# How the first tiles reach TensorE in a fused mixer kernel: layer norm by float32 products and DMA transposes, and w1 by column blocks

## The chip, the cores and the metric

The kernel runs on one core of a Trainium2 chip. The metric is the device time of one launch in microseconds (us), lower being better. Five engines work side by side, each through its own instructions in order: TensorE (PE) multiplies matrices, VectorE (DVE), ScalarE (ACT) and GpSimd (POOL) work elementwise, and SyncE (SP) issues DMAs. Waits between engines are semaphores.

## The reference, cut to what matters

```
x  = A_x                                # 1 x 2048 x 512, float32
xn = layernorm(x)
s  = A(xn)  # qkv = layernorm-ed input @ wqkv (512 x 1536); 32 heads of 16;
            # each position attends to 8 positions, 2 apart; then @ wo (512 x 512)
g  = silu(B(xn))
            # B: y = layernorm(xn); h = gelu(y @ w1 + b1)  (512 x 1376); h @ w2 + b2
out = x + s * g
```

## The kernel before, in words

**Tiles.** Positions are dealt into two classes of 1024, even and odd (the dilation is 2), each of eight tiles of 128 positions. Layer norm is by position, so a tile with positions on the partitions gets its mean and variance from DVE; but for a product with a weight the 512 features must be on the partitions. Each normalized tile is therefore transposed into `yT` (four tensors of four tiles: `yT[0]` and `yT[1]` for class 0, `yT[2]` and `yT[3]` for class 1).

**Precision.** A float32 product is done as three f16 products: every operand is split into a high f16 part and a low one (the remainder), and hi x hi, lo x hi and hi x lo are summed in PSUM. Weights are scaled by a power of two first, which needs a sum of squares over the whole weight (`sumsq`, on ACT), a sum over partitions (`total`, a product with a matrix of fours on PE), and a few tiny DVE steps (`half_exp`, `up`, `down`); then `split` writes the two halves (line 436 the high half on ACT or 434 on DVE, line 437 the low half on DVE).

**Stages.** The work is cut into eight units (class, block of eight heads). `qkv` (lines 611 to 666) multiplies the eight tiles of a class by a 384-column block of wqkv, 12 matmuls a tile (line 632), and ACT evicts each into `U[0]` or `U[1]` in turn (line 648). `attention` (676 on) is DVE and POOL work on `U`. The MLP (`mlp1`, 890 to 932, and `mlp2`, 934 on) runs over four chunks of 512 positions and eleven column blocks of w1 and is spread between the units. Last comes the product with wo (837 on).

**The start.** Tiles of x are loaded in the order of `LOADS` (line 40), between the two halves of wqkv's first block. `ln0` (540 to 583) takes a group of tiles: statistics (`stats`, 525 and 526), the factors (`factors`, 504 to 520, with a power on POOL at 512 and 519), the normalized tile (by DVE at 564 or by ACT at 534), four PE transposes of 128 x 128 into PSUM (571), and copies into the high and low halves of `yT` (581 on ACT, 582 on DVE). Tiles 2 and 3 (`FP`, line 42) also leave a float32 copy (577), and in unit 0 they are multiplied as float32 by the wqkv block as it was loaded (639), so that these products need not wait for its scale. Up to 26 idle matmuls (1042) fill PE before that.

**w1 and w2.** w1 (512 x 1376) lies as four row blocks side by side, [128, 4 x 1376]. It is loaded in four pieces (`W1C`, line 34) from SP's queue, before anything of w2; each is split as a whole (1083 to 1086), with both halves on DVE. A column block of `mlp1` reads from all four row blocks, so its 12 matmuls need all four pieces. w2 follows in two loads of 1 MiB and three of 256 KB (1024 to 1029).

**What sets the order.** The program doesn't run in the order of its text. Every operation is handed to a planner (class `Plan`, line 83) with an engine, an estimated duration, what it reads and writes, and a priority (a lower number first). The planner plays the engines in estimated time (`issue`, line 203): at each step it takes, for the engine that can start earliest, the ready operation of the lowest priority, and this gives each engine's fixed order. Buffers come from rings (`Ring`); a new user waits for the last. Estimates for DMAs are in `place`, and `earliest` limits the planned DMAs in flight. On the chip an engine that reaches a wait in its order holds everything behind it.

Of the kernel before, what the change touches and what calls it, by code (L numbers as in the profile page):

```python
# [33 lines left out]
W1C = [0, 2048, 4096, 5120, KT * F]  # L34
LAG = 2
# [17 lines left out]

DVE_LO = range(0, 44)

# [27 lines left out]
class Plan:  # L83
# [76 lines left out]
    def earliest(self, o):  # L160
        t = max(self.free[o.eng], o.ready)
        if o.port:
            t = max(t, self.portfree)
        if o.eng == "sp" and o.nbytes and len(self.landed) >= QUEUE:
            t = max(t, self.landed[-QUEUE])
        return t

    def place(self, o, t):

        if o.eng == "sp":  # L170
# [6 lines left out]
            self.landed.append(end)  # L177
# [79 lines left out]
MARGIN = {"pe": 0.2, "dve": 0.15, "act": 0.05}  # L257
# [3 lines left out]
QUEUE = 8  # L261

PW2, PS2 = 0.9, 0.74
PWQ1, PW1 = 0.7, 0.75
# [4 lines left out]
WAKE = 4  # L269
WAKE0 = 22  # L270
# [6 lines left out]
PFP = 0.62  # L277
# [13 lines left out]
def tile_mixer(ctx, tc, a_x, a_wqkv, a_wo, b_w1, b_b1, b_w2, out):  # L291
# [34 lines left out]
    ident = sb.tile([P, P], F32, name="ident")  # L326
    make_identity(nc, ident)
    fours = sb.tile([P, P], F32, name="fours")
    nc.vector.memset(fours, 4.0)
    halves = sb.tile([P, 16], F32, name="halves")  # L330
# [8 lines left out]
    w1 = sb.tile([P, 2, KT, F], F16, name="w1")  # L339
# [18 lines left out]
    R_w = Ring(sb, [P, 16], F32, 8, "lw")  # L358
# [27 lines left out]
    def total(dst, dkey, cols, n, ckeys, late=False):  # L386

        b = (R_ps if late else R_z[0]).new()
        if n == 2:
            for k in range(2):  # L390
                pl.add("pe", 0.15, lambda k=k: nc.tensor.matmul(
                    b.t[:, 0:1], fours, cols()[:, k:k + 1], start=(k == 0), stop=(k == 1)),
                    [ckeys[k]], [b], prio=min(pl.prio, PTOT))
            n = 1
        else:
            pl.add("pe", 0.3, lambda: nc.tensor.matmul(b.t[:, 0:n], fours, cols()[:, 0:n], start=True,
                                                       stop=True), ckeys, [b], prio=min(pl.prio, PTOT))
# [62 lines left out]
    def prep_q(hb):  # L460
# [9 lines left out]
        with pl.fuse():  # L470
# [4 lines left out]
            down(qsc[:, hb, 1:2], ("qi", hb), h, 24.0)  # L475
        st = 1 if hb == 0 else 2
# [14 lines left out]
    cpos = [2, 3, 0, 1, 4, 5, 6, 7]  # L491
# [46 lines left out]
    yF = {}  # L538

    def ln0(ii, xs, xkeys):  # L540
        n = len(ii)
        first, way = dict(prio=PLN + pl.prio * 1e-3), dict(prio=PLN + 0.03 + pl.prio * 1e-3)
# [4 lines left out]
        behind = [("yd", i) for i in (2, 3) if n > 1]  # L547
        fz = pl.fuse()
        for a in range(n - 1):
            with pl.fuse():  # L550
                stats(mv, a, mk[a], xs[a], [xkeys[a]] + behind)
        fz.__enter__()
        stats(mv, n - 1, mk[n - 1], xs[n - 1], [xkeys[n - 1]] + behind)
        rb = factors(n, mv, mk, cT[:, 0, cpos[ii[0]]:cpos[ii[0]] + n], [("c", 0, i) for i in ii],
                     ii[0] in ACT_Y, lambda: fz.__exit__(None, None, None), **{"pp": first["prio"]})
        for a, i in enumerate(ii):
            y = R_f.new()
            o = (i % 4) * P
            dst = yT[i // 4]
            if ii[0] in ACT_Y:  # L560
                with prio(PLN + 0.04):
                    y_act(xs[a], rb, a, [xkeys[a]], lambda y=y: y.t, y, ("y_", i))
            else:
                dve(512, lambda a=a, y=y: nc.vector.tensor_scalar(
                    y.t, xs[a](), mv()[:, a, 0:1], rb[0].t[:, a:a + 1], op0=ALU.subtract,
                    op1=ALU.mult), [xkeys[a], (rb[0], 0)] + mk, [y, ("yd", i)], f=0.72, **first)
            b = R_z[1 + i % 3].new()

            def tr(b=b, y=y):
                for k in range(KT):  # L570
                    nc.tensor.transpose(b.t[:, k * P:(k + 1) * P], y.t[:, k * P:(k + 1) * P], ident)
            pe(4, P, tr, [y], [b], fp32=2, **first)
            p3 = lambda b=b: b.t.rearrange("p (k t) -> p k t", k=KT)
            hi, lo = dst[:, 0, :, o:o + P], dst[:, 1, :, o:o + P]
            if i in FP:
                yf = yF[i] = R_L.new()
                act(512, lambda b=b, yf=yf: nc.scalar.copy(yf.t, b.t), [b], [yf], aps=0, **way)
                p3, b, way2 = (lambda yf=yf: yf.t.rearrange("p (k t) -> p k t", k=KT)), yf, dict(prio=PFP)
            else:
                way2 = way  # L580
            act(512, lambda p3=p3, hi=hi: nc.scalar.copy(hi, p3()), [b], [("yh", 0, i)], aps=0, **way2)
            dve(512, lambda p3=p3, hi=hi, lo=lo: nc.vector.tensor_tensor(  # L582
                lo, p3(), hi, op=ALU.subtract), [b, ("yh", 0, i)], [("y", 0, i)], port=i in FP, **way2)

# [651 lines left out]
```

## Time and profile before

| | |
|---|---|
| median of 3 runs | 420.26 us (419.76 to 420.91) |
| the profiled execution | 419.94 us, span 418.2 us from first to last instruction |
| PE busy | 408.5 us, 98% |
| DVE busy | 384.2 us, 92% |
| ACT, POOL busy | 214.8 us, 111.4 us |
| moved by DMA | 44.83 MB, mean 107 GB/s |

An engine's row in the profile gives its busy time; a group of instructions is a line of the kernel, an engine, and output <- input tiles with buffer numbers left out (`ps`, `z` and `pl` are PSUM; `f`, `prod`, `lw`, `s` small SBUF rings). A float32 matmul shows as two instructions, each with its own weight load. In the timeline each row is a start, a length, the engine, the line and how many instructions were merged; brackets give the idle time before it and what ended it. A PE row's length holds the way through the pipeline, so the distance between starts is what a row costs. SPq rows are DMA issues; their landing is given apart.

### The profile page before, as it was taken

The numbers are of one execution on the slowest core, as the hardware profiler recorded it, in microseconds if no ns is written. First come the engines' busy times: TensorE is split into PE (matmuls) and PEld (weight loads), VectorE is DVE, ScalarE is ACT, GpSimd is POOL, SyncE is SP. The second block draws the span as 40 slices with busy tenths as digits, with TensorE's granted clock in tenths as the row PEclk, the third lists the DMA queues.
The fourth block names the chain that finished last, engine by engine and source line by source line (L and its number), as shares of the span: only waits on it lengthen the run. The fifth ranks groups of instructions, "written<-read, shape, count | busy, mean of one in ns | idle before, by whom it ended". The sixth has DMA issues, their size and how long they took to land.

```text
span 418.2 us, 5558 instructions
## 1 busy us (share of the span) xinstructions
PE 408.5 (98%) x2095; PEld 208.7 (50%) x2095; DVE 384.2 (92%) x403; ACT 214.8 (51%) x321; POOL 111.4 (27%) x126
## 2 busy tenths in 40 slices
PE   7799999999999999999999999999999999999995
PEld 4466544444554455445544654465455544444442
DVE  5958999999999999899998999999999998999953
ACT  6799972762539764843396335134212573263500
POOL 5310200004341525042504250433124304520031
PEclk9999999999999999999999999999999999999999
DMA  8963260030036247621271025104505343016132
GB/s 292 415 225 106 77 213 2 16 137 0 0 97 175 72 100 171 135 59 27 71 206 63 2 87 125 52 26 130 184 0 152 117 130 119 2 34 217 27 125 100
DMA packets 42650, 44.83 MB, mean 107 GB/s; under 512 B 27480, under 2 KB 27920, under 8 KB 42112
## 3 DMA queue, kind: packets, MB, share of 16 engines
q1 hardware_dynamic: 42624, 44.49, 35.1%
q8 instruction: 16, 0.26, 0.3%
q14 instruction: 10, 0.08, 0.1%
HBM read 23.53 MB, written 7.34 MB: 74 GB/s over the span
## 4 chain that ended last, share of the span: by engine, by line
PE 81%; DVE 11%; ACT 4%; issue 1%; DMA 1%; SPq 0%; POOL 0%; DVEq 0%
PE ps L632 24%; PE z L943 24%; PE ps L898 22%; PE ps L815 7%; PE z L815 2%; DVE w L437 2%; DVE prod L691 2%; DVE L L694 2%; ACT w L436 1%; DMA prod<-in_A_x_dram 1%; DVE bn L525 1%; PE pl L632 1%; DVE h L921 1%; PE pl L815 1%; DVE w L434 1%
## 5 line engine op out<-in xcount | busy, mean ns | idle before, releaser
L898 PE MATMUL ps<-yT,w 128*128 128x512 f16 (+1 forms) x528 | 120.8, 379 | 0.0
L632 PE MATMUL ps<-wq,yT 128*128 128x384 f16 x708 | 117.9, 326 | 1.0 <-DVE yT L582 1.0
L943 PE MATMUL z<-w,h 128*128 128x512 f16 x480 | 110.8, 379 | 0.0
L632 PEld LDWEIGHTS <-yT 128*128 128x128 f16 x744 | 72.8, 98 | 49.0 <-DVE yT L582 1.3
L898 PEld LDWEIGHTS <-w 128*128 128x128 f16 (+1 forms) x528 | 52.9, 100 | 61.3 <-issue 0.5
L915 ACT ACTIVATE ps<-ps,b1T,hsc 128x512 f32<-128x512 f32 (+1 forms) x44 | 32.8, 748 | 87.1 <-PE ps L898 86.9
L691 DVE TENSOR_TENSOR prod<-U 128x2048 f32<-128x2048 f32 x32 | 73.0, 2285 | 2.8 <-DMA U<-U 1.7
L943 PEld LDWEIGHTS <-h 128*128 128x128 f16 x480 | 47.0, 98 | 55.4
L694 DVE TENSOR_REDUCE L<-prod 128x128 f32<-128x2048 f32 x32 | 72.9, 2280 | 0.4
L648 ACT ACTIVATE U<-ps,cs 128x384 f32<-128x384 f32 x61 | 35.1, 578 | 65.1 <-PE ps L632 63.6
L749 DVE TENSOR_TENSOR prod<-pl,U 128x2048 f32<-128x2048 f32 x28 | 63.2, 2281 | 4.3 <-POOL prod L759 4.2
L759 POOL TENSOR_TENSOR prod<-prod,prod 128x2048 f32<-128x2048 f32 x7 | 31.7, 4528 | 100.0 <-DVE prod L749 100.0
L769 POOL TENSOR_TENSOR prod<-prod 128x1024 f32<-128x1024 f32 x14 | 32.9, 2347 | 0.0
L768 POOL COPY gate<-prod 1x1 f32<-1x1 f32 x21 | 5.5, 263 | 92.7 <-DVE prod L691 89.9
L815 PE MATMUL ps<-wo,oT 128*128 128x512 f16 x132 | 29.6, 379 | 0.0
L921 DVE SCALAR_TENSOR_TENSOR h<-ps,hsc,h 128x512 f16<-128x512 f32 x40 | 29.5, 741 | 0.1
L815 PEld LDWEIGHTS <-oT 128*128 128x128 f16 x189 | 18.5, 98 | 22.1
L918 ACT ACTIVATE h<-ps,hsc 128x512 f16<-128x512 f32 x40 | 27.2, 683 | 0.8
L744 DVE TENSOR_TENSOR prod<-prod,prod 128x2048 f32<-128x2048 f32 x9 | 20.5, 2278 | 0.0
L915 ACT ACT_TABLE_LOAD x11 | 14.1, 1283 | 6.1 <-PE ps L898 5.9
L769 POOL TENSOR_TENSOR prod<-prod,prod 128x1024 f32<-128x1024 f32 x7 | 16.4, 2348 | 0.0
L732 ACT ACTIVATE o<-prod,osc 128x1024 f16<-128x1024 f32 (+1 forms) x9 | 9.5, 1052 | 11.8 <-POOL prod L769 7.4
(155 smaller groups left out, 346.8 us busy)
## 6 DMA issues: line engine op xcount, KB each, us to landing
f<-in_A_x_dram SPq DMA_DIRECT2D x31, 256.0 KB, 3.2
U<-U SPq DMA_DIRECT2D x16, 392.0 KB, 3.8
gd<-f SPq DMA_DIRECT2D x12, 256.0 KB, 2.2
oT<-in_B_w_dram SPq DMA_DIRECT2D x2, 1024.0 KB, 11.9
yT<-in_B_w_dram SPq DMA_DIRECT2D x2, 1024.0 KB, 12.6
f<-gd SPq DMA_DIRECT2D x8, 256.0 KB, 3.2
out_dram<-f SPq DMA_DIRECT2D x8, 256.0 KB, 2.6
out_dram<-U SPq DMA_DIRECT2D x7, 256.0 KB, 2.0
```

The source lines that it names most:

```text
L632: nc.tensor.matmul(b.t[:, 0:384], y[:, s, k, o:o + P], wq[:, hb, t, k], start=(n == 0), stop=(n == 11))
L648: act(384, lambda i=i, b=b: nc.scalar.activation(U3[:, i:i + 31:15, :], b.t[:, 0:384].rearrange("p (t e) -> p t e", t=3), AF.Identity, sca ...
L691: dve(2048, lambda p2=p2, g=g: nc.vector.tensor_tensor(p2(), q, slots(Ut, KH, 2 * g), op=ALU.mult), qk + [("kh", ub, 0), ("kh", ub, 1), (" ...
L694: dve(2048, lambda pr=pr, g=g: nc.vector.tensor_reduce(L3()[:, 2 * g:2 * g + 2], pr.t.rearrange("p (r f d) -> p r f d", r=2, d=DH), AX.X, ...
L749: dve(2048, lambda: nc.vector.tensor_tensor(pr.t.rearrange("p (r f d) -> p r f d", r=2, d=DH), A3()[:, 2 * g:2 * g + 2].rearrange("p r (f ...
L759: pool(4.75, lambda: nc.gpsimd.tensor_tensor(acc.t, acc.t, p1.t, op=ALU.add), [acc, p1], [acc])
L769: nc.gpsimd.tensor_tensor(x.t[:, 0:1024], x.t[:, 0:1024], y(), op=ALU.add)
L815: nc.tensor.matmul(b.t, oT[:, hb, i // 4, s, i % 4], wo[:, t, hb], start=(hb == 0 and n == 0), stop=(hb == last and n == 2))
L898: nc.tensor.matmul(b.t[0:M], w1[:, s, k, f * P:f * P + M], yT[ch][:, t, k], start=(n == 0), stop=(n == 11))
L915: act(512, lambda: nc.scalar.activation(b.t[0:M], b.t[0:M], AF.Gelu_apprx_tanh, bias=b1T[0:M, f:f + 1], scale=hsc[0:M, 1:2]), [b, ("b1T",) ...
L921: dve(512, lambda: nc.vector.scalar_tensor_tensor(lo()[0:M], b.t[0:M], hsc[0:M, 2:3], hi()[0:M], op0=ALU.mult, op1=ALU.subtract), [b, hk], ...
L943: nc.tensor.matmul(z.t, hl[s][0:K, t * P:(t + 1) * P], w2[0:K, w, f], start=(f == 0 and n == 0), stop=(f == NF - 1 and n == 2))
```

## The change

The host passes a further input, `A_xt`: tiles 4 to 7 of class 0 with the features already on the partitions, 256 KB each. The loads become t4, t5, the two halves of wqkv's first block, x0, x1, t6, x2, x3, t7, x4 to x7 (t for a transposed tile, x for a plain one; all eight plain tiles are still loaded, one at a time).

`FP` is now (4, 5, 6, 7). For each of these, `center` sums a transposed tile over its four row blocks (DVE for tiles 4 and 5, POOL for 6 and 7), takes the mean over the partitions by a float32 product with a matrix of 1/512, and subtracts it in place on DVE. `direct` multiplies the centred tile as float32 by the unscaled wqkv block, four matmuls of 384 columns each. The factor 1/standard deviation is not applied to the tile: it is put into the scale `cs` of the eviction in unit 0.

For all eight tiles `y0` makes the normalized tile in place (ACT for tiles 0, 2, 3, 4, DVE for 1, 5, 6, 7), casts its high half (on the same engine), subtracts for the low half on DVE, and SP issues a DMA transpose of both halves into `yT`. The PE transposes, their identity matrix and the copies out of PSUM are gone. Unit 0 takes the tiles in the order 4, 5, 6, 7, 0, 1, 2, 3, of which 0 to 3 are f16 products from `yT`; the other units take 1 to 7 and then 0.

w1 lies as eleven column blocks one after another, each with its four row blocks inside. It is still loaded in four pieces, now issued by ACT: piece n after the transpose of tile n has landed. It is split in seven parts (`W1P`): the first two of one column block each, with the high half on DVE; then five with the high half on ACT, with a priority behind the MLP's own steps. A column block of `mlp1` waits for its own part alone. w2's two large loads are issued by ACT after the transposes of tiles 5 and 7.

`total` uses bf16 matrices of fours and the upper 16 bits of the sums. The planner limits planned DMAs in flight by bytes instead of by number, and several priorities are renamed or moved. A branch for the MLP's low half that no step took (lines 927 to 931) and its diagonal matrix (1081) are removed.

```diff
-GROUPS = [(2,), (3,), (0, 1), (4, 5), (6, 7)]
-LOADS = [(2, 1), "q0", "q2", (3, 1), (0, 2), (4, 2), (6, 2)]
-FP = (2, 3)
-ACT_Y = (0, 1, 4, 5)
-W1DVE = (0, 1, 2, 3)
+W1P = [(0, 1), (1, 2), (2, 4), (4, 6), (6, 8), (8, 10), (10, 11)]
+W1FIRST = 2
+FP = (4, 5, 6, 7)
+XC = FP
+GROUPS = [(0, 1), (2, 3), (4, 5, 6, 7)]
+LOADS = [("t", 4), ("t", 5), ("q", 0), ("q", 2), ("x", 0), ("x", 1), ("t", 6), ("x", 2), ("x", 3), ("t", 7),
+         ("x", 4), ("x", 5), ("x", 6), ("x", 7)]
+XT = (0, 4, 30, 34)
+Y_ENG = {0: "act", 1: "dve", 2: "act", 3: "act", 4: "act", 5: "dve", 6: "dve", 7: "dve"}
+W1ENG = ["dve", "dve", "act", "act", "act", "act", "act"]
...
+    mean1 = sb.tile([P, P], F32, name="mean1")
+    nc.vector.memset(mean1, 1.0 / D)
...
+    xt = {i: U[1][:, XT[n] * P:(XT[n] + 4) * P].rearrange("p (k t) -> p k t", k=KT) for n, i in enumerate(FP)}
+    def center(i):
...
+        if n < 2:
+            dve(512, lambda: nc.vector.tensor_reduce(f3()[:, 0], x3.rearrange("p k t -> p t k"), AX.X, ALU.add),
+                [("xt", i)], [f], port=False)
+        else:
+            pool(0.75, lambda: nc.gpsimd.tensor_tensor(f3(), x3[:, 0:2], x3[:, 2:4], op=ALU.add), [("xt", i)], [f])
+            pool(0.45, lambda: nc.gpsimd.tensor_tensor(f3()[:, 0], f3()[:, 0], f3()[:, 1], op=ALU.add), [f], [f])
+        pe(1, P, lambda: nc.tensor.matmul(b.t[:, 0:P], mean1, f3()[:, 0], start=True, stop=True), [f], [b], fp32=6, prio=0.04)
+        m = lambda: b.t[:, 0:P].rearrange("p (o t) -> p o t", o=1).to_broadcast([P, KT, P])
+        dve(512, lambda: nc.vector.tensor_tensor(x3, x3, m(), op=ALU.subtract), [b, ("xt", i)], [("xc", i)], port=False)
...
+    def direct(i):
+        b = pb[i] = (([R_pl] + R_z[1:] + [R_ps] * 4)[FP.index(i)]).new()
+        for k in range(KT):
+            pe(1, 384, lambda k=k: nc.tensor.matmul(
+                b.t[:, 0:384], xt[i][:, k], stq[0]()[:, k * 384:(k + 1) * 384], start=(k == 0), stop=(k == KT - 1)),
...
+    def y0(i, a, mv, mk, rb):
...
+        dma(P * 2048, lambda: nc.sync.dma_start_transpose(
+            dst.rearrange("p a k t -> p (a k) t")[:, :, o:o + P], y16.t.bitcast(F16)),
+            [y16, (y16, 0)], [("yh", 0, i), ("y", 0, i)], rate=1e6, issue=1.3, tail=2.6)
...
-    IORD, IORD0 = [2, 3, 1, 4, 5, 6, 7, 0], [2, 3, 0, 1, 4, 5, 6, 7]
+    IORD, IORD0 = [1, 2, 3, 4, 5, 6, 7, 0], [4, 5, 6, 7, 0, 1, 2, 3]
...
-                nc.tensor.matmul(b.t[0:M], w1[:, s, k, f * P:f * P + M], yT[ch][:, t, k],
+                nc.tensor.matmul(b.t[0:M], w1[:, s, f * 512 + k * M:f * 512 + (k + 1) * M], yT[ch][:, t, k],
...
+    def behind(nbytes, fn, r, w):
+        pl.add("act", 0.4, fn, r, w, nbytes=nbytes)
...
+            behind(P * 4 * (b - a), lambda a=a, b=b: nc.scalar.dma_start(s1[n]()[:, a:b], b_w1[:, W1C[n] + a:W1C[n] + b]),
+                   [W1AFTER[n]], [key])
...
+    W1AFTER = [("y", 0, 0), ("y", 0, 1), ("y", 0, 2), ("y", 0, 3)]
...
+        behind(P * 8192, lambda: nc.scalar.dma_start(s2a, b_w2[:, 0:4]), [("y", 0, 5)], [("yT", 2), ("s2", 0)])
+        behind(P * 8192, lambda: nc.scalar.dma_start(s2b, b_w2[:, 4:8]), [("y", 0, 7)], [("yT", 3), ("s2", 1)])
...
+    lay["A_xt"] = inputs["A_x"].reshape(P, NI, DIL, KT, P)[:, list(FP), 0].transpose(1, 3, 2, 0)
...
+    w1 = inputs["B_w1"].reshape(KT, P, F)
+    lay["B_w1"] = _np.concatenate([w1[:, :, f * P:(f + 1) * P].transpose(1, 0, 2).reshape(P, -1) for f in range(NF)], 1)
```

More of the change, by code (lines that the diff above doesn't have):

```diff
@@ L275 @@
 PQLO = 0.55
-PFP = 0.62
+PFPLN = 0.35
 U1MH = 4
@@ L545, in ln0 @@
         mk = [(mvb, a) for a in range(n)]
-        behind = [("yd", i) for i in (2, 3) if n > 1]
-        fz = pl.fuse()
-        for a in range(n - 1):
+        for a, i in enumerate(ii):
             with pl.fuse():
[L551 to L555, printed above, removed]
@@ L636, in qkv @@
             if u == 0 and i in FP:
-                yf = yF[i]
-                for k in range(KT):
-                    pe(1, 384, lambda k=k, b=b, yf=yf: nc.tensor.matmul(
-                        b.t[:, 0:384], yf.t[:, k * P:(k + 1) * P], stq[hb]()[:, k * 384:(k + 1) * 384],
-                        start=(k == 0), stop=(k == KT - 1)), [yf, ("stq", hb, k)], [b], fp32=4.1,
-                       holds=stkey[hb], after=pl.users([b] + [("v", ub, i)]))
                 ends = []
```

246 lines of the change are left out of this document (130 added, 116 removed).

## The prediction

> **What bounds the kernel now.** I read the page's busy line and chain first, then the busy time by stage, cut at 20.70 us, where TensorE (PE) last waited.
>
> ```profile
> span 418.2 us, 5558 instructions
> PE 408.5 (98%) x2095; PEld 208.7 (50%) x2095; DVE 384.2 (92%) x403; ACT 214.8 (51%) x321; POOL 111.4 (27%) x126
> PE 81%; DVE 11%; ACT 4%; issue 1%; DMA 1%; SPq 0%; POOL 0%; DVEq 0%
> ```
>
> ```profile
> 5.80:20.70 14.90, 11.59 (x55) 6.72 (x55) 13.40 (x49) 12.07 (x23) 5.19 (x7) 1.00 1.03 402
> 20.70:48.74 28.04, 28.04 (x182) 18.04 (x183) 20.60 (x46) 27.35 (x50) 3.71 (x3) 1.00 0.37 128
> 48.74:400.62 351.88, 351.54 (x1778) 175.18 (x1776) 341.23 (x289) 172.89 (x247) 94.18 (x100) 1.00 0.32 91
> ```
>
> The columns are the stretch, its length, then busy us of PE, PEld, DVE, ACT and POOL, the clock, the DMA share and GB/s. From 20.70 us on PE is busy in 28.04 of 28.04 and 351.54 of 351.88 us: the kernel is PE's list of work, laid end to end. It can end earlier only if that dense stretch starts earlier or holds less. The granted clock is 1.00 throughout, so work has a fixed price. The timeline of PE shows the start, and the chain the transposes inside the dense part:
>
> ```profile
> 7.13 2.20 PE L639 MATMUL ps<-prod,L 128*128 128x384 f32 x6 [0.21 <-ACT L L577]
> 11.31 2.85 PE L639 MATMUL ps<-prod,L 128*128 128x384 f32 x8
> 13.99 0.38 PE L1042 MATMUL z<-fours 128*128 128x256 bf16 x2
> 18.96 1.48 PE L632 MATMUL ps<-wq,yT 128*128 128x384 f16 x8 [1.02 <-DVE yT L582]
> 48.74 7.93 PE L898 MATMUL ps<-yT,w 128*128 128x512 f16 x36
> ```
>
> ```profile
> 20.70 1.09 PE z L571 x8
> ...
> 22.45 0.64 PE z L571 x4
> ...
> 25.04 0.44 PE z L571 x4
> ...
> 32.90 1.95 PE ps L632 x12
> ```
>
> Two float32 tiles are multiplied from 7.13 us; the second takes 11.31 to 13.99 = 2.68 us. An f16 tile (12 matmuls) takes 1.95. By 20.70 two float32 tiles and one f16 tile are done; five f16 tiles of unit 0 and eight of unit 1 remain: 13 x 1.95 = 25.4 us. With 1.09 + 0.64 + 0.44 = 2.17 us of transposes and about 0.5 of totals that fills the 28.04 us until the MLP starts at 48.74.
>
> **The change, part by part: when data lands.** The loads are a stream of bytes; the first users and the SP queue show when it reached each point. In the SP rows each issue waits for the landing of an earlier load, in order: tiles 0-1 (8.85), 4-5 (10.19), 6-7 (11.52), then w1's first two pieces (14.02, 16.52).
>
> ```profile
> 3.35 0.69 DVE L525 BATCH_NORM_STATS2 bn<-prod 128x6 f32<-128x512 f32 x1 [2.35 <-DMA prod<-in_A_x_dram]
> 4.58 0.84 ACT L465 ACTIVATE wq<-prod 128x768 bf16<-128x768 f32 x1 [2.57 <-DMA prod<-in_A_wqkv_dram]
> 6.63 0.69 DVE L525 BATCH_NORM_STATS2 bn<-prod 128x6 f32<-128x512 f32 x1 [0.66 <-DMA prod<-in_A_x_dram]
> 8.85 0.33 SPq L1015 DMA_DIRECT2D h<-in_B_w_dram  x1
> 10.19 0.33 SPq L1024 DMA_DIRECT2D yT<-in_B_w_dram  x1
> 11.52 0.33 SPq L1025 DMA_DIRECT2D yT<-in_B_w_dram  x1
> 14.02 0.33 SPq L1026 DMA_DIRECT2D b1T<-in_B_b_dram  x1
> 16.52 2.35 SPq L1029 DMA_DIRECT2D f<-in_B_w_dram  x3
> ```
>
> So 0.25 MiB are in at 3.35, 0.625 at 4.58, 1.25 at 6.63, 1.75 at 8.85, 2.25 at 10.19, 2.75 at 11.52, 3.75 at 14.02. Laid over the new order: t4 3.35, t5 4.2, wq's halves 5.4 and 6.6, x0 7.7, x1 8.85, t6 9.5, x2 10.2, x3 10.85, t7 11.5, x4 to x7 by 14.0, q1 (0.75 MiB) at 15.9.
>
> **Durations**, from the groups, the transposes' own view (issue and landing), the list of DMA issues (median us to landing last) and the page:
>
> ```profile
> L582 DVE TENSOR_TENSOR yT<-z,yT 128x512 f16<-128x512 f32 x6 | 3.9, 680 | 1.6 <-ACT yT L581 1.6
> L525 DVE BATCH_NORM_STATS2 bn<-prod 128x6 f32<-128x512 f32 x8 | 5.4, 681 | 3.0 <-DMA prod<-in_A_x_dram 3.0
> L564 DVE TENSOR_SCALAR f<-prod,lw,lw 128x512 f32<-128x512 f32 x4 | 2.1, 543 | 0.1
> L534 ACT ACTIVATE f<-prod,lw 128x512 f32<-128x512 f32 x4 | 3.3, 813 | 0.1
> L581 ACT CAST yT<-z 128x512 f16<-128x512 f32 x6 | 3.3, 574 | 0.4 <-PE z L571 0.4
> L383 ACT ACTIVATE w<-oT 128x2048 bf16<-128x2048 f32 x2 | 3.8, 1906 | 0.0
> L604 SPq DMA_TRANSPOSE yT<-f x8: 1232/1244/1300, 145.1 to 189.1; - x8
> DMA to landing us min/median/max: 3.0/3.1/3.1
> f<-in_B_w_dram SPq DMA_DIRECT2D x3, 256.0 KB, 9.1
> L769 POOL TENSOR_TENSOR prod<-prod 128x1024 f32<-128x1024 f32 x14 | 32.9, 2347 | 0.0
> ```
>
> *Float32 products.* Centring t4: a strided DVE sum over 512 elements. No row has that stride; it is bounded by 0.54 (the fastest DVE pass of this size above) and 1.4 (twice the 0.68 of the statistics, if the stride halves the rate); I take 0.68, the nearest row's. Then a 128-column float32 product with the 1/512 matrix (between one 0.14 us transpose pass and half a 0.67 us product step; I take 0.4), then a subtraction of 0.68: 3.35 + 0.68 + 0.5 + 0.68, and t5's sum between, is 5.5 us. wq's first half is there at 5.4. Tiles 4 and 5: 2 x 2.68, to 10.9. Tile 6 is summed on POOL: 384 elements at 2.29 ns and two starts, 1.1; 9.5 + 1.1 + 0.5 + 0.7 = 11.9, so PE idles 1.0 us. Tile 6 runs to 14.7, tile 7 (centred by 14.0) with its mean product to 17.6. A doubled DVE sum moves all of this by under 0.8, which the 1.0 us gap before tile 6 mostly swallows.
>
> *f16 tiles through the DMA.* x1's statistics end near 9.8, factors and POOL's power near 11.4; tile 0 is normalized by ACT (0.3 + 0.81), cast (0.57), and its low half subtracted on DVE (0.68) behind tile 1's work: about 14.6. The transpose is issued at 14.6, on SP behind loads that land by 15.9, and 3.1 us later, 17.7 to 19.0, the tile is there; I take 18.0. The others follow at the SP queue's 1.25 to 1.3 us each, or as DVE finishes them (tile 3's low half by about 17): faster than PE's 1.95. The landing under load isn't in the trace: from 3.1 to the 9.1 us of the 256 KB loads queued at the start. I take 3.1, since w1 now waits for the transposes and leaves the queue nearly empty. SP's own order gains 14 instead of 7 early issues (0.4 each) and eight transposes (1.25); nothing due before 26 us stands behind them except b1 and w2, not due until the MLP.
>
> *The sum.* PE is dense from 18.0 with 4 + 8 f16 tiles, 12 x 1.95 = 23.4, and 0.3 of totals (bf16 now, one pass instead of two; worth 0 to 0.7 overall). The MLP starts at 41.7 instead of 48.74: **7.0 us**. The two extra float32 tiles cost 5.4 us of PE, but in 5.5 to 17.6, where 14.90 us held waits and filler matmuls.
>
> *Does w1 keep up?* Its pieces are issued by ACT, each behind a wait for one tile's landing (18 to 22 us); behind those waits in ACT's order stand evictions, unit 1's wq scaling and the sums of squares. At 2.50 us per MiB (14.02 to 16.52) its 2.69 MiB are in by 26. ACT's squares take 1.9 twice, by size about 1.0 and 0.5, and their reads, 6.1; with evictions and wq's scaling between, they end near 32. The first two column blocks (about 0.4 + 0.6 us each on DVE) are split by 35, seven us before they're due. In the run before, every row block had to be split before the first MLP column, and that ended at 47.7, one us ahead of need:
>
> ```profile
> 47.10 0.61 DVE L437 SCALAR_TENSOR_TENSOR w<-h,hsc,w 128x384 f16<-128x384 f32 x1
> ```
>
> *Other engines.* DVE gains two sums, four subtractions and four casts (1.4 + 2.7 + 2.2 at the row's 0.54) and loses five of w1's seven high halves (about 2.9) and 0.65 for the diagonal: +2.8, covered by its 7.4 us idle in 20.70 to 48.74. ACT loses ten copies (5.7) and gains four casts (2.3), five high halves (about 5) and six DMA issues (0.4 each): +4. ACT has only 0.7 us idle in that stretch, but the later high halves are due one MLP step after another, where ACT is half busy (172.89 of 351.88). If that cover fails it costs up to 3 us. At the other end the last unit's output:
>
> ```profile
> 396.70 0.75 DVE L734 SCALAR_TENSOR_TENSOR o<-prod,osc,o 128x512 f16<-128x512 f32 x1 [0.79 <-ACT o L732]
> 403.38 9.71 PE z L815 x45
> 413.09 0.67 PE z L865 x6
> ```
>
> DVE ends that chain at 397.45 and its transpose lands 3.1 later, near 400.6; the 24 products that need it are 5.2 us (45 take 9.71), and 4.4 follow after PE's last (413.76 to 418.2). So even a DVE that gained nothing would let the span fall to 410.2. DVE doesn't take the 7 us back.
>
> The profiled run took 419.94 us around its span of 418.2; less 7.0 it is 412.9, and against the median of 420.26, **413.2**.
>
> A rule speaks against the part by DMA. The Trainium skill, "VectorE: DVE Perf Modes", section "Rules for kernel authors", says to transpose 128x128 on TensorE where PSUM will do; its "The three transpose paths" gives 1309 ns a block for the DMA. An estimate from that page, with eight blocks a tile one by one, is 10.5 us; the trace's 3.1 us for a whole tile disagrees, and the sum stays.
>
> **Rivals.**
>
> *Tiles arrive one by one.* If transposes don't overlap, they land every 3.1 us: 18, 21.1, 24.2, 27.3. Unit 0 ends at 29.3 instead of 25.8; tiles 4 to 7 land by 39.7 and are due from 35.1 to 41, so no more is lost. 3.5 us are saved: 416.7. For it: every transpose row was issued alone or in a pair, so overlap isn't shown. Against: the issue takes 1.25 and each landing is 3.1 even in a pair.
>
> *Transposes stand behind w1: slower.* Each landing releases a w1 piece into the same 16 DMA engines, already shown full (1.03) until 20.70. If a transpose waits out the piece released before it, 2.5 us per MiB, the landings are 5.6 us apart: 18, 23.6, 29.2, and 33.5 behind the half piece. Unit 0 ends at 35.5 and unit 1 at 51.1, 2.4 late; w2's two MiB among tiles 4 to 7 add about 1.2. Near 423.9. It turns slower when the landings are over 4.3 us apart (18 + 3g + 1.95 = 25.8 + 7). For it: 9.1 us for queued 256 KB loads. Against: those stood behind 2 to 3 MiB on SP's own queue, while w1 moves to ACT's. The Trainium skill, "DMA: Bandwidth & Descriptors", section "Issuing engines are not separate DMA queues", says that DMAs of all issuers interleave on the same engines: by it the sharing is real, though interleaving is less than waiting out; no row before shows two issuers.
>
> *ACT gives it back.* The MLP starts early but its split weights don't: w2's squares (6 us) and splits, plus the 4 us added, keep PE waiting until the old place of 48.7. About 420, no change. Against: w1 and w2 land at or before their old need.
>
> **How the numbers follow.** Forecast 0.64, own range 411 to 415.5 (the dense start between 16.5 and 20). One by one 0.16 at 416.7. Behind w1 0.14 at 423.9. ACT 0.06 at 420. The range 410.5 to 418 takes in the first two with ACT stalls to 3 us and an early start with cheaper totals, and leaves out the rest. A measurement here tells about 0.3%, 1.3 us: faster 0.80, within 0.06, slower 0.14.
>
> **What would show it.** The first centred product near 5.5; the fourth float32 tile done near 17.6; transposes landing 1.3 to 2 us apart; the first MLP matmul near 41.7; PE idle under 1 us between 18 and 400. A landing over 4 us apart, ACT waiting long at its DMA issues, or PE waiting on w1 or w2 after 41 would make the forecast wrong.

## The result, and the profile after

The changed kernel takes **439.06 us** (median of 4 runs, 435.1 to 439.97) against 420.46 us of the kernel before in the same session: a ratio of 1.0426, 95% interval 1.0359 to 1.0492. It is slower by 18.6 us, where 7 us less were forecast. The profiled execution took 438.48 us around a span of 436.7.

The page of the changed kernel, its busy line and its chain by engine:

```profile
span 436.7 us, 5474 instructions
PE 412.4 (94%) x2048; PEld 206.8 (47%) x2048; DVE 385.5 (88%) x403; ACT 216.5 (50%) x320; POOL 111.5 (26%) x124
...
PE 85%; DMA 8%; DVE 4%; ACT 1%; issue 1%; SPq 0%; DVEq 0%; ACTq 0%
```

PE's work didn't grow much (408.5 to 412.4 us); its idle time did, and DMA went from 1% to 8% of the chain. The stretches say where (columns as in the prediction: PE, PEld, DVE, ACT, POOL, clock, DMA share, GB/s):

```profile
5.80:20.70 14.90, 12.84 (x48) 7.32 (x48) 12.72 (x41) 10.42 (x21) 5.59 (x8) 1.00 0.85 301
20.70:70.00 49.30, 34.13 (x159) 17.21 (x157) 27.26 (x57) 29.06 (x49) 4.28 (x3) 0.79 0.82 183
```
```profile
70.00:400.00 330.00, 328.98 (x1677) 164.36 (x1676) 317.68 (x276) 169.19 (x242) 93.20 (x99) 1.00 0.33 90
```

From 70 us on PE is dense at clock 1.00, as before. Between 20.70 and 70 it stands idle for 49.30 - 34.13 = 15.2 us, where the kernel before had no idle time, and the mean clock there is 0.79. PE's waits from 5 to 75 us name what it waited for (us in total, times, longest):

```profile
PE pl L661 <- DMA yT<-f: 8.7, 2, 5.7
PE ps L661 <- DMA yT<-f: 3.3, 1, 3.3
PE z L570 <- DVE U L563: 1.8, 2, 1.1
```

`yT<-f` are the new transposes: 12.0 us of waits by themselves; the third row is the float32 tiles' centring, which falls before 20.70. The other 3.2 of the 15.2 us are waits for w1's total (until 47.12), its scale (48.62) and its first split (50.17). The timeline of PE (start, length; the brackets give the idle time before a row):

```profile
6.82 1.53 PE L570 MATMUL pl<-prod,U 128*128 128x384 f32 x4 [0.26 <-DMA prod<-in_A_wqkv_dram]
...
18.19 2.85 PE L570 MATMUL z<-prod,U 128*128 128x384 f32 x8 [1.12 <-DVE U L563]
20.88 0.19 PE L395 MATMUL z<-s,fours 128*128 128x1 bf16 x2
24.39 8.91 PE L661 MATMUL ps<-wq,yT 128*128 128x384 f16 x36 [3.32 <-DMA yT<-f]
36.28 3.24 PE L661 MATMUL pl<-wq,yT 128*128 128x384 f16 x12 [2.98 <-DMA yT<-f]
39.31 2.72 PE L661 MATMUL ps<-wq,yT 128*128 128x384 f16 x12
...
56.24 4.02 PE L661 MATMUL pl<-wq,yT 128*128 128x384 f16 x12 [5.68 <-DMA yT<-f]
```

The float32 products end at 20.88. Then PE waits three times for a transposed tile, and each time the matmuls behind the wait run slowly: three tiles in 8.91 us (at 1.95 each they would be 5.85), one in 3.24, the last in 4.02. The transposes themselves (the view of their line), SP's first four in the timeline, and two of ACT's six issues:

```profile
L607 SPq DMA_TRANSPOSE yT<-f x8: 1254/1455/4256, 17.0 to 43.9; - x8
...
DMA to landing us min/median/max: 6.5/10.6/12.3
```
```profile
16.96 8.41 SPq L607 DMA_TRANSPOSE yT<-f  x4
```
```profile
16.72 0.38 ACTq L1032 DMA_DIRECT2D oT<-in_B_w_dram  x1
...
44.14 0.34 ACTq L1065 DMA_DIRECT2D yT<-in_B_w_dram  x1
```

The profile gives the landing of four of the eight transposes: 6.5, 9.1, 12.1 and 12.3 us after their issue, where those into `yT` in the kernel before took 3.0 to 3.1. (Its transposes into `oT`, line 737, took 3.1 to 4.8, a row that the prediction didn't use.) The ACT rows are the loads of w1 (L1032) and w2 (L1065). The first megabyte of w1 is issued at 16.72, ahead of the first transpose at 16.96: "after the transpose of tile n" was an order in the planner's time, not a wait on the chip. The same holds for w2: its loads went out at 44.14 and 44.89, while the last transpose, issued at 43.91, landed at 56.19. So the loads run beside the transposes. Over 31 to 33 us, while the transposes issued at 24.12 and 29.47 are on their way, the queues moved (packets, MB, share):

```profile
q10 hardware_dynamic: 95, 0.45, 91.7%
q1 hardware_dynamic: 235, 0.06, 14.2%
```

q10 is ACT's queue, with 0.45 MB in 95 packets; q1 is SP's, where the transposes travel in many small packets: 0.06 MB in 235.

**Theories.** A: the transposes are late because large loads of ACT's queue run at the same time. B: a run of DMA transposes in this kernel is late by itself. C: whatever the transposes do, the new front holds as much work, or other waits, as it saves.

### The profile page after: what moved, and what is told of

It is laid out like the page before. It is cut to its first block, busy times and chain, and to the rows that moved or that the text cites. A ratio compares the mean times of both kernels' runs of the same rounds, so it can differ in the third digit from the quotient of the medians.

```text
span 436.7 us, 5474 instructions
## 1 busy us (share of the span) xinstructions
PE 412.4 (94%) x2048; PEld 206.8 (47%) x2048; DVE 385.5 (88%) x403; ACT 216.5 (50%) x320; POOL 111.5 (26%) x124
## 4 chain that ended last, share of the span: by engine, by line
PE 85%; DMA 8%; DVE 4%; ACT 1%; issue 1%; SPq 0%; DVEq 0%; ACTq 0%
PE z L954 25%; PE ps L918 25%; PE ps L661 24%; PE ps L838 7%; DMA yT<-f 6%; PE z L838 2%; PE pl L661 2%; DMA prod<-in_A_x_dram 1%; DVE bn L534 1%; DMA gd<-f 1%; DVE f L605 1%; PE pl L838 1%; ACT f L970 0%; ACT L970 0%; ACT L935 0%
## 5 line engine op out<-in xcount | busy, mean ns | idle before, releaser
L918 PE MATMUL ps<-yT,w 128*128 128x512 f16 (+1 forms) x528 | 122.3, 380 | 2.1 <-DVE s L406 1.2
L671 ACT ACTIVATE U<-ps,cs 128x384 f32<-128x384 f32 x58 | 33.6, 579 | 67.9 <-PE ps L661 67.5
L838 PEld LDWEIGHTS <-oT 128*128 128x128 f16 x189 | 18.5, 98 | 22.1
L661 PE MATMUL pl<-wq,yT 128*128 128x384 f16 x24 | 7.3, 484 | 8.7 <-DMA yT<-f 8.7
```

Source lines behind the costliest of these rows:

```text
L661: nc.tensor.matmul(b.t[:, 0:384], y[:, s, k, o:o + P], wq[:, hb, t, k], start=(n == 0), stop=(n == 11))
L671: act(384, lambda i=i, b=b: nc.scalar.activation(U3[:, i:i + 31:15, :], b.t[:, 0:384].rearrange("p (t e) -> p t e", t=3), AF.Identity, sca ...
L838: nc.tensor.matmul(b.t, oT[:, hb, i // 4, s, i % 4], wo[:, t, hb], start=(hb == 0 and n == 0), stop=(hb == last and n == 2))
L918: nc.tensor.matmul(b.t[0:M], w1[:, s, f * 512 + k * M:f * 512 + (k + 1) * M], yT[ch][:, t, k], start=(n == 0), stop=(n == 11))
```

## The experiments

Each was timed against the kernel before beside it (420.47 to 420.99 us); all but `phases` have four runs of their own.

### w_on_sp: the same loads from SP's queue

```diff
-            behind(..., lambda a=a, b=b: nc.scalar.dma_start(s1[n]()[:, a:b], ...),
+            behind(..., lambda a=a, b=b: nc.sync.dma_start(s1[n]()[:, a:b], ...),
-        behind(P * 8192, lambda: nc.scalar.dma_start(s2a, b_w2[:, 0:4]), ...
+        behind(P * 8192, lambda: nc.sync.dma_start(s2a, b_w2[:, 0:4]), ...
```

> The changed kernel, with the four loads of w1 and the two large loads of w2 issued by SP in the same planned order, so that they stand behind the transposes in the same queue. Theory A (a transpose is slow because w1 and w2 come in from the other issuer's queue at the same time): the transposes of tiles 0 to 3 land about 3 to 4 us after their issue instead of a median of 10.6, PE waits under 2 us on them, and the time falls to 412 to 418 us. Theory B (the transposes are slow by themselves in this stretch, whoever issues the loads): landings stay near 9 to 12 us and the time stays within 3 us of 439. If loads in front in the same queue hold transposes too, tiles 4 to 7, which stand behind w1 here, are late by up to 7 us and the time is 420 to 428.

Measured: **424.26 us**, ratio 1.009 (1.0063 to 1.0117). The landing of its transposes, and PE where its f16 tiles start:

```profile
L607 SPq DMA_TRANSPOSE yT<-f x8: 1261/1331/3461, 16.7 to 36.6; - x8
DMA to landing us min/median/max: 3.5/4.6/6.0
```
```profile
20.64 0.19 PE L395 MATMUL z<-s,fours 128*128 128x1 bf16 x2
20.90 2.94 PE L661 MATMUL ps<-wq,yT 128*128 128x384 f16 x17
...
37.89 0.16 PE L400 MATMUL z<-s,fours 128*128 128x4 bf16 x1 [1.95 <-ACT w L386]
...
39.40 1.03 PE L918 MATMUL ps<-yT,w 128*128 128x512 f16 x2 [1.15 <-DVE s L406]
...
41.34 3.99 PE L661 MATMUL pl<-wq,yT 128*128 128x384 f16 x12
```

The same bytes and the same transposes. The edit names only the issuer of six loads, but with the queue goes their time: w1's loads now go out at 22.3 to 25.9 us, behind the first four transposes, where ACT had issued them at 16.7 to 36.3. PE goes from the float32 products straight on to tile 0 (20.64 to 20.90) and never waits for a transpose. 14.8 of the 18.6 us are gone: theory A holds for these. The time is above the 412 to 418 us expected of it; it lies in the range of the third case, but not for that case's reason, since no transpose is waited for. What is left, 3.8 us, fits theory C: PE now waits for w1's sum of squares (`z L400 <- ACT w`, 1.95) and for the scale that comes of it (1.15).

### phases: the transposes and the loads by themselves

This kernel computes nothing of the reference. It issues four transposes of a tile's size, six ways, twice over.

```diff
+        nc.scalar.dma_start(big[0], w[:, 0:2048])          # 52: beside ACT's 1 MiB, 8 KB rows
+        for i in range(4):
+            nc.sync.dma_start_transpose(dst[i], src[i])
```

> Not the reference's computation: it leaves everything out except seven stages of DMAs, done twice, each stage after the one before has landed: four transposes of 128x1024 f16 alone (L40); behind a 1 MiB load on SP (L44); ahead of one on SP (L47); beside a 1 MiB load of 8 KB rows issued by ACT (L52); beside two such loads (L57); beside a 1 MiB load of 2 KB rows issued by ACT (L61); and two loads without transposes, one on each queue. Theory A: landings of 3 to 5 us in L40 and L47, over 8 us in L52 and L57, less in L61 than in L52 if the size of the other queue's packets sets the share; the two plain loads together take about as long as their bytes, 5 to 7 us. Theory B: L40 already shows landings that grow to 9 us or more for the fourth transpose.

Landing of each line's eight transposes, min/median/max (the profile's rows, with the stage ahead of each in words): line 40 alone, line 44 behind a load of 1 MiB on SP's own queue:

```profile
L40 SPq DMA_TRANSPOSE dst<-src x8: 1232/1302/1341, 2.0 to 100.4; - x8
DMA to landing us min/median/max: 3.1/3.3/3.3
```
```profile
L44 SPq DMA_TRANSPOSE dst<-src x8: 1231/1322/3807, 14.5 to 115.0; - x8
DMA to landing us min/median/max: 3.1/4.5/6.3
```

Line 52 beside 1 MiB from ACT's queue in rows of 8 KB, line 61 beside 1 MiB from ACT in rows of 2 KB (line 57, beside two loads of 8 KB rows, landed in 3.2/7.1/12.9):

```profile
L52 SPq DMA_TRANSPOSE dst<-src x8: 1232/1287/1549, 37.6 to 136.2; - x8
DMA to landing us min/median/max: 3.2/6.3/11.8
```
```profile
L61 SPq DMA_TRANSPOSE dst<-src x8: 1232/1277/1503, 72.1 to 167.4; - x8
DMA to landing us min/median/max: 3.2/4.8/6.5
```

Four in a row alone land in 3.3 us at 1.3 us from issue to issue, so they overlap: with `w_on_sp`, theory B falls, and so does the rival "Tiles arrive one by one". Ahead of a load in the same queue (line 47) they land in 3.1 to 3.4. Behind one the worst is 6.3. The medians of lines 52, 57 and 61 say little: ACT's load went out some 3.4 us after the first transpose, so that the first two of each four (3.2 to 3.5 us) hardly met it. The other two land in 9.1 to 11.8 beside rows of 8 KB, and in 6.4 to 6.5 when the rows are a quarter as long.

The load suffers too: the same 1 MiB lands in 5.3 to 5.8 us ahead of or behind the transposes on SP's queue (lines 42 and 48), and in 8.3 and 11.2 beside them from ACT's (line 50). This is more than a sharing of the engines: from 42.5 to 46.0 us, with two transposes and the load on their way, both queues together moved 0.24 MB, 70 GB/s. Two such loads on the two queues without a transpose moved 280 GB/s (87.5 to 95.0 us) and landed in 7.0 to 7.5.

### w_wait: the loads made to wait

```diff
+ (nc.scalar.copy(s1[n]()[0:1, a:a + 1], yT[0][0:1, 1, KT - 1, 511:512]),
   nc.scalar.dma_start(s1[n]()[:, a:b], ...))
-    W1AFTER = [("y", 0, 0), ("y", 0, 1), ("y", 0, 2), ("y", 0, 3)]
+    W1AFTER = [("y", 0, 3)] * 4
```

ACT copies one element of transposed tile 3 into the place to be loaded, so that each load really waits (w2's likewise for tile 7). Tiles 4 to 7 are transposed later, though, so that w1's loads, issued from 32.58 us on, still run beside theirs.

> The changed kernel, with a real wait before each load that ACT issues: ACT copies one element of the transposed tile 3 (for w2 of tile 7) into the load's target first, so that no weight is in flight beside a transpose. Theory A: each landing is 3 to 4.5 us after issue, the MLP's first matmul comes at 42 to 46 us instead of 48.6 and then without the 5.7 us gap, the time is 413 to 421 us; w1 lands later, near 30 us. Theory B: landings stay near 9 to 12 us, and with w1 later still the time is 440 us or more.

Measured: 431.94 us, 1.0258 (1.0211 to 1.0305), where theory A had been given 413 to 421. The landings, and PE's longest waits:

```profile
L607 SPq DMA_TRANSPOSE yT<-f x8: 1242/1359/6206, 19.5 to 43.1; - x8
...
DMA to landing us min/median/max: 3.5/7.7/12.0
```

```profile
PE z L400 <- ACT w L386: 6.2, 1, 6.2
...
PE ps L400 <- ACT junk L386: 1.7, 1, 1.7
```

The profile gives two landings: 3.5 us for one issued at 20.9, with no load beside it, and 12.0 for one issued at 33.3, beside w1. In one kernel, then, both of theory A's cases. PE waits only 0.5 us for transposes, but 6.2 for the squares of the w1 that now comes late, and 1.7 for those of b1 behind them. Letting the loads wait, as the prediction had read the change, gives back 7 us and pays the rest elsewhere. The float32 products also ended 2.5 us later (23.37) in this run: the first started 1.0 us later (7.81), on wq's first half, and the clock then stood at 0.50 from 9 to 11 us. Why wq landed later wasn't found.

### pe_tr, pe_tr_sp and front_alone: the transposes back on PE

`pe_tr` is the changed kernel with four PE transposes a tile and the copies out of PSUM, as before; `pe_tr_sp` has also the loads of w1 and w2 on SP; `front_alone` has also w1 in row blocks. In the last one only the four centred float32 tiles, the bf16 totals and the order around them are left of the change.

```diff
-        dma(P * 2048, lambda: nc.sync.dma_start_transpose(...), ...)
+        for k in range(KT):
+            nc.tensor.transpose(b.t[:, k * P:(k + 1) * P], x()[:, k * P:(k + 1) * P], ident)
```

> The changed kernel with the eight DMA transposes undone: the normalized tiles are transposed by PE into PSUM and copied into the two halves of yT by ACT and DVE, as before; the float32 products of tiles 4 to 7, the column blocks and the loads issued by ACT stay. Theory A and theory B both put the loss in the transposes: 410 to 416 us. If instead the loads issued by ACT, the later w1 or the split by column blocks cost the time, it stays above 425 us.

> The kernel after with TensorE's transposes in place of the DMA's (as in pe_tr, 426.66 us), and w1's and w2's loads issued by SP in place of ACT. If ACT's issuing costs something only where DMA transposes or x's loads are beside it, there is little left to gain: 425.5 to 427. If w1's share of the engines still delays wq's second unit or the scaling that PE waits for (3.8 us of waits in pe_tr): 422 to 424.

> The front alone: the kernel after with TensorE's transposes, w1's and w2's loads by SP and w1 in row blocks, so that of the change only the four transposed, centred float32 tiles, the bf16 totals and the order around them stay. From the measured end of the float32 products (21.4 us in pe_tr), twelve f16 tiles of 1.95 us and 4.3 us of transposes fill PE to 49.1 us, where before reaches 48.7: 420 to 421, no gain, if the front holds as much work as it saves and nothing else is late. If ACT's list (four more casts, the squares) is what keeps PE waiting in the first 50 us: 424 to 427. If the forecast's 4 us of saved waits are there: 416 to 418.

Measured: `pe_tr` 426.66 us, 1.0142 (1.0107 to 1.0177); `pe_tr_sp` 425.64, 1.0112 (1.0091 to 1.0132); `front_alone` 427.36, 1.0152 (1.0131 to 1.0172). The first was expected at 410 to 416: missed, and with it falls the thought that the front gains what the transposes then lose. ACT's issuing costs 1.0 us here, where no DMA transpose is beside it, and with runs of `pe_tr` from 424.67 to 428.02 that isn't resolved. And the front alone is 6.7 us slower than the kernel before. Its stretch and waits:

```profile
20.70:70.00 49.30, 43.42 (x243) 24.07 (x242) 40.80 (x61) 38.42 (x65) 4.47 (x7) 0.97 0.41 137
```
```profile
PE ps L660 <- ACT wq L494: 1.9, 2, 1.6
PE z L573 <- DVE U L566: 1.8, 2, 1.2
PE ps L920 <- DVE w L444: 1.2, 1, 1.2
```

PE is idle for 49.30 - 43.42 = 5.9 us of a stretch that had no idle time before. The longest single wait is on ACT, and ACT's own timeline shows what stood ahead of the scaling of wq that PE needed at 33:

```profile
29.51 1.90 ACT L389 ACTIVATE w<-oT 128x2048 bf16<-128x2048 f32 x1
...
31.59 0.57 ACT L670 ACTIVATE U<-pl,cs 128x384 f32<-128x384 f32 x1
32.06 1.75 ACT L494 ACTIVATE wq<-U,qsc 128x768 f16<-128x768 f32 x2
```

A square of w1 (1.90 us, with no idle time after it) is ahead of the wq scaling in ACT's fixed order: ACT sets this wait. The rest of the 5.9 us is spread over seven waits of 0.2 to 1.2 us on DVE and ACT.

### before_w_on_act and before_cols: one part put into the kernel before

```diff
-        dma(..., lambda: nc.sync.dma_start(s1[n](), b_w1[:, W1C[n]:W1C[n + 1]]),
+        dma(..., lambda: nc.scalar.dma_start(s1[n](), b_w1[:, W1C[n]:W1C[n + 1]]),
```

(and w2's two loads likewise); `before_cols` has w1 by column blocks with the seven-part split, and nothing else of the change.

> The kernel before, with its four loads of w1 and the two large ones of w2 issued by ACT instead of SP; no transposes by DMA run beside them. Theory A (it is the pair, a transpose on one queue beside loads on the other, that is slow): 419 to 422 us, no difference. If loads from ACT's queue were slow as such, w1 lands later and the time rises by 3 us or more.

> The kernel before, with one part of the change alone: w1 by column blocks, split in seven parts, five high halves on ACT. Theory A: PE was dense before its first MLP matmul anyway, so within 1 us of the kernel before (419.5 to 421.5). If the later splits on ACT cost the MLP its early steps, 422 to 425.

Measured: `before_w_on_act` 425.21 us, 1.0102 (1.0086 to 1.0118), where no difference was expected. There are no early transposes in it; PE's longest wait and its first float32 product show what was hurt:

```profile
PE z L571 <- DVE f L564: 3.5, 1, 3.5
```
```profile
12.48 4.00 PE L639 MATMUL ps<-prod,L 128*128 128x384 f32 x6
```

In the kernel before that product is at 7.13. On SP's queue w1 is issued from 4.09 us on and comes behind x and wq. On ACT's its first two pieces go out at 0.73 and run beside them: DVE gets the first tile of x at 6.29 instead of 3.35 us, and ACT the first half of wq at 9.72 instead of 4.58. `before_cols`: 423.25 us, 1.0059 (1.004 to 1.0077): the column blocks by themselves cost 2.3 us. PE's first 48.7 us look as before; after that come waits of 0.4 to 1.2 us on DVE, ACT and a DMA.

### sp_rows: the column blocks taken back

`w_on_sp` with w1 in four row blocks, each split as a whole on DVE.

```diff
-    for m, (f0, f1) in enumerate(W1P):
+    for n in range(4):
+        c0, c1 = W1C[n:n + 2]
```

> The kernel after with w1's and w2's loads issued by SP (as in w_on_sp, 424.26 us) and with w1 back in row blocks: four row blocks, each split as a whole on DVE, no column blocks. The front and the transposes by DMA stay. Theory that the column blocks cost the same 2.3 to 2.8 us here as they did alone in before_cols (423.25 against 420.4): 421.5, near before. The forecast's view that column blocks are what lets the MLP start early, since all four row blocks have to be split before its first column: PE waits 2 to 4 us for w at the MLP's start, 426 to 428.

Measured: 429.4 us, 1.0205 (1.0188 to 1.0222), 5.1 us above `w_on_sp` and above both ranges expected. Behind this front the column blocks are worth having, as the prediction held. But the wait for w at the MLP's start that was expected isn't what the trace shows: the largest wait is for a transpose, landing in 4.5 to 6.0 us, of which the last was issued at 38.5 instead of 36.6.

```profile
PE pl L661 <- DMA yT<-f: 3.2, 1, 3.2
```

### fill and sp_replanned: two attempts to win back the rest

`fill` puts 38 idle bf16 matmuls into the two totals of `w_on_sp`, where PE waits and its clock falls. `sp_replanned` tells `w_on_sp`'s planner measured durations instead.

```diff
+                for _ in range(fill):
+                    nc.tensor.matmul(b.t[:, 0:2 * P], fours[:, 0:P], fours, start=True, stop=True)
```
```diff
-                [("xt", i)], [f], port=False)
+                [("xt", i)], [f], port=False, f=1.75)
-            [y16, (y16, 0)], [("yh", 0, i), ("y", 0, i)], rate=1e6, issue=1.3, tail=2.6)
+            [y16, (y16, 0)], [("yh", 0, i), ("y", 0, i)], rate=1e6, issue=1.3, tail=3.6)
-        pl.add("act", 0.4, fn, r, w, nbytes=nbytes)
+        pl.add("act", 0.4, fn, r, w, nbytes=nbytes, rate=400e3, tail=5.0)
```

(Tile 4 is also normalized on DVE instead of ACT.)

> The run with w1 and w2 on SP's queue, with 38 idle matmuls added on PE in front of the two totals at which it waited, some 4 us of work in a wait of the same length. If the half clock after an idle PE is a cost of its own, the matmuls at 41 to 45 us take their full-speed time and the time falls by 1.5 to 2.5 us to 422 to 423; if the clock costs nothing there, since the next data isn't ready either, it stays at 424 or rises.

> The run with w1 and w2 on SP's queue, with the planner told the durations that its trace showed: the strided sum 0.98 us, a transpose's landing 1 us later, w1's landing 3.6 us later; and tile 4 normalized by DVE. PE then takes five of unit 1's tiles before the totals of w1 instead of three. Theory A (of the 3.8 us that the run on SP's queue still stands above the kernel before, most is PE standing in its fixed order at w1's total, and the half clock after it): PE has no wait over 1 us between 21 and 60 us, the granted clock stays 1.00, and the time falls by 4 to 7 us to 417 to 420 us. Theory C (the front itself holds more work than it saves: four float32 tiles that end at 20.7 us): PE's dense stretch begins where it did before and the time stays at 422 us or more.

Measured: `fill` 425.37 us, 1.0123 (1.007 to 1.0176). The clock is 1.00 from 20.70 to 70, up from 0.93 in that stretch of `w_on_sp`, and the time isn't lower: by 47.5 us PE is 0.9 us ahead of `w_on_sp`, and then it waits 1.8 us for an ACT eviction, where it had waited 0.6. No gain from the clock is seen in this place; with runs from 423.45 to 427.73, and a filler that holds the second total back (40.17 against 38.09), the test is no sharper than that. `sp_replanned` 433.0 us, 1.0277 (1.0241 to 1.0313): 8.7 us worse than `w_on_sp` (8.2 against the kernels before beside them), with its waits on the squares (2.9 and 2.6 us) and on wq (2.1). No kernel tried here beat the kernel before.

| kernel | transposes in unit 0 | w1, w2 issued by | w1 blocks | us |
|---|---|---|---|---|
| before | PE | SP | rows | 420.5 |
| before_w_on_act | PE | ACT | rows | 425.21 |
| before_cols | PE | SP | columns | 423.25 |
| front_alone | PE, new front | SP | rows | 427.36 |
| pe_tr_sp | PE, new front | SP | columns | 425.64 |
| pe_tr | PE, new front | ACT | columns | 426.66 |
| sp_rows | DMA, new front | SP | rows | 429.4 |
| w_on_sp | DMA, new front | SP | columns | 424.26 |
| after | DMA, new front | ACT | columns | 439.06 |

The parts don't add up singly: ACT's issuing costs 4.2 us in the kernel before, 1.0 in the new front with PE transposes and 14.8 with DMA transposes; column blocks cost 2.3 in the kernel before and gain 1.7 and 5.1 in the new front.

## Why the prediction was wrong

**The step that failed: "I take 3.1, since w1 now waits for the transposes and leaves the queue nearly empty."** Both halves were wrong. On the chip w1's first piece didn't wait for a transpose: it was issued at 16.72, before the first one. And the landings were 6.5 to 12.3 us, two of the four known ones beyond the 9.1 that was kept as the upper bound. The code says `behind`, with a read of `("y", 0, n)`, and I took a read in the planner's list for a wait on the chip. `w_on_sp` shows what it was worth: 14.8 us by the queue and the order that comes with it.

**The mechanism was among the rivals, and undersized.** "Transposes stand behind w1" gave 423.9. It priced the delay as one piece of w1 waited out (5.6 us between landings) and set against itself that w1 moves to another queue. The runs show the opposite sign of that argument: behind a load in the same queue a transpose lands in at most 6.3 us, beside the same load from the other queue in 9.1 to 11.8 (`phases`; with all loads on SP in `sp_replanned`, up to 8.3). Its sum also let PE wait at full clock; after each wait the matmuls ran at about half.

The Trainium skill, "DMA: Bandwidth & Descriptors", section "Queues, rings and completion order", says that each DMA engine takes turns between the queues that have work, a packet at a time. By that rule the queue with small packets moves fewer bytes a turn; the bytes of 31 to 33 us (0.45 MB against 0.06 MB) and the shorter delay beside 2 KB rows agree in direction. The counts don't (95 packets against 235, where equal turns would give equal numbers), but whether a packet of the profile is what the page calls one isn't shown. And turns alone don't explain the loss: from 26 to 28 us the two queues moved 0.07 MB together, with a transpose on its way, and in `phases` 70 GB/s. Why both queues slow down together stays open.

**The dense start.** Forecast at 18.0, with tile 0 there; it was 24.39 here, and 20.90 in `w_on_sp`, where the float32 products set it. These were forecast to end at 17.6 and ended at 20.9, the second step that was mis-sized, by 3.3 us:

```profile
3.44 1.96 DVE L556 TENSOR_REDUCE f<-U 128x128 f32<-128x512 f32 x2 [2.17 <-DMA U<-in_A_xt_dram]
...
14.44 0.75 POOL L560 TENSOR_TENSOR f<-f 128x128 f32<-128x128 f32 x1
...
17.46 0.68 DVE L563 TENSOR_TENSOR U<-U,ps 128x512 f32<-128x512 f32 x1
```

The strided sum took 0.98 us, inside its bounds of 0.54 and 1.4. wq's first half arrived at 6.8, not 5.4, so the first product started 1.3 us late (6.82 against 5.5). Most of the rest is tile 7, "centred by 14.0": POOL's second sum for it ran at 14.44, behind the powers for the factors, and DVE's subtraction at 17.46, behind two low halves, so that it was ready at 18.14. I had charged the operations and not the queue in front of them. (Tile 6's sum there, 9.5 + 1.1 + 0.5 + 0.7, is 11.8 and not 11.9, which changes nothing.)

**PE's list.** The 7.0 us, less these 3.3, are 3.7 us. That much was really saved: `w_on_sp` has PE idle for 49.30 - 44.39 = 4.9 us from 20.70 to 70 and about 1.9 us lost to the half clock in the tile at 41.34, 6.8 in all, yet its span is only 3.1 longer than before, so the work left on its list at 20.70 is about 3.7 us shorter. (Short rows at half clock, some 0.5 us, aren't counted.)

```profile
20.70:70.00 49.30, 44.39 (x230) 22.73 (x229) 40.76 (x76) 42.24 (x70) 4.79 (x7) 0.93 0.85 241
```

For the changed kernel the same sum goes: 15.2 us idle, 6.5 at half clock (by the distances between starts: three tiles in 8.8 instead of 5.85, then one each in 3.0, 2.6 and 3.8 instead of 1.95), and 0.7 more idle after 70, less 3.7, is 18.7 against a measured 18.5 of span. (`fill` says that the two losses aren't independent: where the clock is kept up, a wait can take its place.) The saving goes with the transposes that left PE: with them back on PE (`front_alone`) nothing remains of it.

**w1.** The squares were to end near 32 and the first column blocks to be split by 35, "seven us before they're due". In `w_on_sp` the squares ended at 37.8 and PE waited for their total from 35.9; in the changed kernel the total came at 47.1. ACT's squares stood ahead of work that PE needed, and the totals stood in PE's fixed order, so PE waited for both. The column blocks were worth 5.1 us beside DMA transposes (`sp_rows`), though the wait for splits that the prediction gave as the reason isn't in that trace.

**"ACT gives it back"** was priced at the old time, as if PE could wait no longer than before. The front alone passes that by 6.7 us: a fixed order can wait in more places than the one that it had replaced. That wrong estimates made this order bad isn't shown: planned with measured durations (`sp_replanned`) it was slower still.

What was right: that PE's dense list is the bound (from 70 to 400 us it is idle for under 2 us in every kernel here), the transposes' overlap when alone, the f16 tile at 1.95 us, and that DVE's end doesn't set the time.

What stays open: why a transpose and a load from the other queue slow each other so far, and which of the new front's 5 to 6 us of small waits could be ordered away. The one attempt, `sp_replanned`, made them worse.

## What to carry to other kernels

A late load on a second issuer's queue isn't behind anything: it shares the DMA engines with whatever the first queue is moving, and in these runs the DMA transposes, with their small packets, suffered most; keep bulk prefetch on the queue whose order protects the urgent transfers, or make it wait by a semaphore (and see whether it then comes too late itself, as in `w_wait`), and look in the list of issues for the real time. When a transfer replaces work on the bound engine, price its landing under the traffic that will really be there; a trace in which it always ran alone gives only the lower bound. In a kernel with a fixed order, a step that becomes late by a few us holds up everything that was placed behind it, so a saving at the start has to be larger than the waits that it opens.

## What the runs showed of the hardware that was not expected

- **Two queues and a transpose.** Alone 3.1 to 3.3 us; behind 1 MiB in its own queue up to 6.3; beside 1 MiB from the other queue 9.1 to 11.8 with 8 KB rows and 6.4 to 6.5 with 2 KB rows; beside two loads of 8 KB rows up to 12.9. The loads slow down too, 8.3 and 11.2 against 5.3 to 5.8 us, and for some us both queues together move 70 GB/s.
- **Loads on the other queue overtake.** With no DMA transposes at the start, moving six loads from SP to ACT cost 4.2 us, since w1 ran beside x and wq instead of behind them. The Trainium skill, "DMA: Bandwidth & Descriptors", section "Issuing engines are not separate DMA queues", says that DMAs of all issuers interleave on the same engines and that several issuers only save issue time; the first half agrees, and `before_w_on_act` shows that the second leaves out a cost.
- **The clock changes on a grid of 3.41 us.** In the changed kernel PE idles from 21.07 to 24.39; by windows of 1 us:

```profile
23.00:24.00 1.00, 0.00 (x0) 0.00 (x0) 0.90 (x7) 0.26 (x1) 1.00 (x2) 0.73 0.46 86
24.00:25.00 1.00, 0.61 (x2) 0.28 (x3) 1.00 (x3) 0.93 (x2) 0.52 (x1) 0.50 1.29 267
...
31.00:32.00 1.00, 1.00 (x9) 0.59 (x7) 0.65 (x1) 0.90 (x2) 0.00 (x0) 1.00 1.09 329
```

The clock's column (third from the end) goes over 0.73 to 0.50, stays there until 30, and is back at 1.00 in 31 to 32. In windows of 0.05 us the fall is at 23.46 and the return at 30.29; the next fall is at 37.11, its return at 40.53, and one more pair at 50.77 and 61.01. All six lie whole multiples of 3.41 us apart. So the clock fell 2.4 us into the first idle stretch, but 0.8 us after the end of the second (33.30 to 36.28), and it came back 5.9, 4.2 and 4.8 us after PE had resumed. The Trainium skill, "TensorE: Matmul & The Clock Gate", section "Part 1: The HAM clock gate (the "warmup" mystery)", has the clock halved after an idle window of about 3.4 us and restored after about as long a busy one; the spacing here agrees. But the 3.41 us before the first two falls weren't wholly idle: PE worked for 1.0 and 0.8 us of them.
